# Three low bits of each 64-bit weight: from a VectorE instruction to a second GpSimd instruction

## The chip, the core and the metric

The kernel runs on one core of one Trainium2 chip. The metric is the device time of one execution in microseconds. Engines are named as the profile names them: PE is TensorE's matmul and PEld its weight load, DVE is VectorE, ACT is ScalarE, POOL is GpSimd, SP is SyncE, whose queue issues most loads.

## What is computed

Attention with a learned position bias, and behind it a feed-forward layer of two matrix products. The 2304 tokens are 4 batches of 576; there are 8 heads of 64.

```python
scores = scale * np.matmul(q, k.transpose(0, 1, 3, 2))
x = (psi_rel / psi_i)[..., None]            # from the positions alone
bias = np.maximum(x @ w1 + b1, 0.0) @ w2    # 576 x 576 for each head
scores = scores + bias.transpose(2, 0, 1)[None]
...
attn = attn / (np.sum(attn, axis=-1, keepdims=True) + 1e-09)
attn_out = np.matmul(attn, v)
...
h = x @ w_in                                # 512 -> 2048
g = h * np.clip(h + 3.0, 0.0, 6.0) / 6.0
out = g @ w_out                             # 2048 -> 512
```

The weights `w_in` and `w_out` arrive as 64-bit floats. The chip reads them as pairs of 32-bit words and builds 32-bit floats from them.

## The kernel before

**The 64-bit weights.** `w_in` is worked through in 8 chunks of 128 x 1024 numbers (`w_in_prep`), `w_out` in 8 more (`w_out_prep`). A chunk is 1 MB, and lies in SBUF as 1024 pairs (low word, high word) in each partition. One chunk takes these steps: a load on SP's queue (L242); on ACT the absolute value of the high word, scaled so that the exponent of a 64-bit float becomes that of a 32-bit one (L252, into the staging tile `u`); on POOL the high word times 0, which leaves only its sign, +0 or -0, in place (L253); and then on DVE `f64_pack`, three instructions: L260 clamps `u` and takes its maximum, L263 shifts `u` left by three bits and ORs the sign into it, L266 shifts the low word right by 29 bits and ORs its three top bits in. Then the chunk is scaled by a power of two and split into two f16 parts: the high part on ACT (L123) and the low part on DVE (L140). For the first two chunks of `w_out` POOL does two of these steps (L128, L133).

For `w_in` the chunks land in two buffers named `w` by turns, and the staging tile is the space of `wo`. For `w_out` they land by turns in two parts of `wo` and in `z_e`, and `u` is `cu`.

**What surrounds it.** The program has three stretches. First the position bias is made in 36 groups of 16 rows: z on DVE (L846) and ACT (L850), a matmul (L863), the evacuation on ACT (L879, `bo`), and a store to DRAM from ACT's queue (L885). Eight groups make the first bias table of 128 rows, which is loaded back (`bt<-bias`, L488) before the first softmax. Alongside run the eight chunks of `w_in` and the first attention tiles: the scores plus bias and the row minimum of the negative on DVE (L559), exp on ACT (L570), a transpose on PE (L618) evacuated by ACT (L621). When the last chunk of `w_in` is done, DVE computes the ratios of its rows (L216, `r_w1c`) and the first feed-forward block begins: h on PE (L781), relu on ACT (L771), the product on DVE (L764), the f16 split on ACT (L758) and POOL (L760). The eight chunks of `w_out` are made in this second stretch. Its end is the ratios of `w_out` (L216 again, `r_w2c`), with which the stored g of the first block are scaled (L121, L123); then the second product of the block begins (L804, `o_ps`). From there on, the third stretch, attention and feed-forward blocks alternate on PE to the end.

**What sets the order.** Every engine runs its instructions in the order of the program, and that order is made by a scheduler at build time from the priorities of the code and its own idea of how long things take. So a change of one instruction also moves others.

## Time and profile before

| | before |
|---|---|
| device time, median of 3 runs | 695.44 us (695.28 to 698.04) |
| span of the profiled execution, first to last instruction | 690.7 us |
| PE busy in it | 640.2 us (93%) |
| DVE busy | 486.6 us (70%) |
| ACT busy | 487.5 us (71%) |
| POOL busy | 261.1 us (38%) |

The profile is of one execution. It lists its span but no time of its own; by the median, 4.7 us lie around the span. A busy engine is one that has an instruction running; matmuls are pipelined, so a busy PE is not one at its peak. A line such as L266 is a line of the kernel before.

### The profile page before, as it was taken

The numbers are of one execution on the slowest core, as the hardware profiler recorded it, in microseconds if no ns is written. First come the engines' busy times: TensorE is split into PE (matmuls) and PEld (weight loads), VectorE is DVE, ScalarE is ACT, GpSimd is POOL, SyncE is SP. The second block draws the span as 40 slices with busy tenths as digits, with TensorE's granted clock in tenths as the row PEclk, the third lists the DMA queues.
The fourth block names the chain that finished last, engine by engine and source line by source line (L and its number), as shares of the span: only waits on it lengthen the run. The fifth ranks groups of instructions, "written<-read, shape, count | busy, mean of one in ns | idle before, by whom it ended". The sixth has DMA issues, their size and how long they took to land. (4 is left out here: it accounts for less than half of the span.)

```text
span 690.7 us, 15099 instructions
## 1 busy us (share of the span) xinstructions
PE 640.2 (93%) x5552; PEld 453.1 (66%) x5552; DVE 486.6 (70%) x1150; ACT 487.5 (71%) x970; POOL 261.1 (38%) x322
## 2 busy tenths in 40 slices
PE   7688899787899999899989999999999999999998
PEld 2234456564587667578878877777767777777775
DVE  7889977999737977577778777876688668731310
ACT  7986768987739977697568857886688657832620
POOL 1111125756114532255335634653265425420420
PEclk9998999998999999999999999999999999999999
DMA  8899769651856798979999989787968795730000
GB/s 295 297 329 345 263 246 366 234 194 32 259 162 147 188 251 178 256 180 196 237 266 232 232 186 206 149 184 154 242 123 184 159 198 120 114 66 25 1 10 28
DMA packets 175737, 130.13 MB, mean 188 GB/s; under 512 B 137520, under 2 KB 144944, under 8 KB 174640
## 3 DMA queue, kind: packets, MB, share of 16 engines
q1 hardware_dynamic: 165872, 113.84, 66.0%
q10 hardware_dynamic: 9792, 15.34, 7.4%
q8 instruction: 43, 0.70, 0.4%
q14 instruction: 30, 0.25, 0.1%
HBM read 77.24 MB, written 15.34 MB: 134 GB/s over the span
## 5 line engine op out<-in xcount | busy, mean ns | idle before, releaser
L781 PE MATMUL h_ps<-x,wi 128*128 128x256 f16 (+1 forms) x1536 | 200.9, 288 | 8.7 <-DVE t L764 6.0
L804 PE MATMUL o_ps<-g,wo 128*128 128x256 f16 (+1 forms) x1536 | 195.5, 286 | 2.0 <-ACT g L123 1.3
L781 PEld LDWEIGHTS <-wi 128*128 128x128 f16 x1536 | 147.4, 98 | 60.9 <-issue 20.1
L804 PEld LDWEIGHTS <-wo 128*128 128x128 f16 x1536 | 147.3, 98 | 47.4 <-issue 10.5
L760 POOL TENSOR_TENSOR g<-t,g 128x256 f16<-128x256 f32 (+1 forms) x128 | 105.6, 834 | 154.9 <-ACT g L758 153.4
L570 ACT ACTIVATE bt<-bt,sm 128x576 f32<-128x576 f32 x144 | 110.6, 768 | 57.0 <-DVE sm L559 53.7
L140 DVE SCALAR_TENSOR_TENSOR hl<-bt,sm,hl 128x576 f16<-128x576 f32 x112 | 99.2, 900 | 30.1 <-ACT hl L123 14.7
L764 DVE SCALAR_TENSOR_TENSOR t<-t,t,h_ps 128x320 f32<-128x320 f32 (+1 forms) x112 | 56.0, 515 | 40.3 <-ACT t L771 39.2
L117 POOL TENSOR_SCALAR hl<-bt,sm 128x576 f16<-128x576 f32 x56 | 47.4, 847 | 94.9 <-DVE sm L582 30.1
L758 ACT ACTIVATE g<-t 128x256 f16<-128x256 f32 (+1 forms) x128 | 55.4, 438 | 31.8 <-DVE t L764 30.9
L559 DVE CUSTOM_DVE_ANT_0 bt<-s_ps,bt 128x576 f32<-128x576 f32 x88 | 64.5, 751 | 10.8 <-PE s_ps L527 5.4
L771 ACT ACTIVATE t<-h_ps,t,hr 128x320 f32<-128x320 f32 (+1 forms) x112 | 64.1, 586 | 6.1 <-PE h_ps L781 4.2
L413 POOL TENSOR_TENSOR qkl<-st,qkh 128x576 fp32r<-128x576 f32 (+2 forms) x48 | 57.9, 1229 | 24.3 <-ACT qkh L406 18.6
L863 PE MATMUL b_ps<-z_e,w_sb 128*32 128x288 f32 x448 | 45.1, 430 | 12.3 <-ACT bo L879 5.1
L814 ACT ACTIVATE ot<-o_ps,os 128x256 f32<-128x256 f32 (+1 forms) x32 | 15.9, 496 | 56.6 <-PE o_ps L804 51.4
L123 ACT ACTIVATE hl<-bt,sm 128x576 f16<-128x576 f32 x56 | 43.0, 770 | 7.2 <-DVE sm L582 4.2
L578 DVE TENSOR_SCALAR sm<-sm 128x1 f32<-128x1 f32 x112 | 16.7, 150 | 44.4 <-ACT bt L570 44.0
L846 DVE TENSOR_SCALAR z_e<-T,nbp 128x576 f32<-128x576 f32 x69 | 39.6, 622 | 11.6 <-PE b_ps L863 11.5
L879 ACT ACTIVATE bo<-b_ps,cv_sb,isc 128x288 f32<-128x288 f32 (+1 forms) x54 | 35.7, 663 | 2.9 <-DMA bias<-bo 2.0
L863 PEld LDWEIGHTS b_ps<-z_e,w_sb 128*32 128x32 f32 x448 | 14.8, 111 | 32.3 <-ACT z_e L850 6.6
L253 POOL TENSOR_SCALAR w<-w 128x1024 f32<-128x1024 f32 x8 | 10.8, 1348 | 65.3 <-ACT wo L252 52.9
L850 ACT ACTIVATE z_e<-T,bp 128x576 f32<-128x576 f32 x43 | 32.4, 771 | 3.9 <-DVE bp L1037 2.9
(125 smaller groups left out, 902.1 us busy)
## 6 DMA issues: line engine op xcount, KB each, us to landing
bt<-bias SPq DMA_DIRECT2D x36, 576.0 KB, 5.3
bias<-bo ACTq DMA_DIRECT2D x36, 288.0 KB, 5.6
w<-in_w_in_dram SPq DMA_DIRECT2D x8, 1024.0 KB, 7.2
vs<-in_vp_dram SPq DMA_DIRECT2D x24, 320.0 KB, 5.0
st<-in_qk_dram SPq DMA_DIRECT2D x16, 448.0 KB, 4.5
wo<-in_w_out_dram SPq DMA_DIRECT2D x5, 1024.0 KB, 5.1
bt<-bias SPq DMA_DIRECT2D x16, 288.0 KB, 3.6
qk<-in_qkd_dram SPq DMA_DIRECT2D x8, 544.0 KB, 8.9
```

The source lines that it names most:

```text
L117: nc.gpsimd.tensor_scalar(out=out, in0=full, scalar1=scale, scalar2=1.0, op0=ALU.mult, op1=ALU.mult)
L140: nc.vector.scalar_tensor_tensor(out=out, in0=full, scalar=scale, in1=high, op0=ALU.mult, op1=ALU.subtract)
L413: nc.gpsimd.tensor_sub(out=lo[:, c:c + w], in0=t[:, c:c + w], in1=hi[:, c:c + w].bitcast(F32))
L559: nc.vector.tensor_tensor_reduce(out=halves(bt), in0=ps, in1=halves(src), op0=ALU.add, op1=ALU.min, scale=-0.125, scalar=3.0e38, accum_out ...
L570: nc.scalar.activation(out=bt, in_=bt, func=AF.Exp, scale=-1.0, bias=sm[:, 0:1], accum_out=total)
L758: nc.scalar.activation(out=g[:, 0], in_=uu, func=AF.Copy)
L760: e.tensor_sub(out=g[:, 1], in0=uu, in1=g[:, 0])
L764: nc.vector.scalar_tensor_tensor(out=t_t[f], in0=t_t[f], scalar=cols(f)[2], in1=h_t.pop(f)[:, 0:n], op0=ALU.min, op1=ALU.mult,)
L771: nc.scalar.activation(out=t_t[f], in_=h_t[f][:, 0:n], func=AF.Relu, scale=cols(f)[0], bias=cols(f)[1],)
L781: nc.tensor.matmul(out=h_t[f][:, 0:n], lhsT=wi[:, a, c, f * 128:(f + 1) * 128], rhs=x[:, e, c], start=(k == 0), stop=(k == 3 * KC - 1),)
L804: nc.tensor.matmul(out=ops[:, 0:n], lhsT=wo[:, a, f, e * 128:(e + 1) * 128], rhs=g_t[f][:, r], start=(f == 0 and a == 0 and r == 0), stop= ...
L863: nc.tensor.matmul(out=pss[a][32 * k:32 * k + 32, 0:HALF], lhsT=w2_sb, rhs=z[:, a * HALF:(a + 1) * HALF],)
```

## The change

The instruction L266 on DVE is taken out. In its place POOL gets a second instruction behind the one that makes the sign. It reads the chunk as 16-bit numbers: the upper half of the low word (`lo`, every fourth 16-bit number), multiplies it by 7.499/65535, and writes the rounded result, a number from 0 to 7, as a 16-bit number into the lower half of the high word (`low`), beside the sign. The OR of L263 then puts sign and three low bits in at once.

```diff
+LOW3 = 7.499 / 65535
...
     def f64_abs(t, u):
         if len(t.shape) == 3:
             tv, u = t.rearrange("p a (c w) -> p a c w", w=2), u.rearrange("p (a c) -> p a c", a=2)
-            lo, hi = tv[:, :, :, 0], tv[:, :, :, 1].bitcast(F32)
+            t16 = t.bitcast(U16).rearrange("p a (c w) -> p a c w", w=4)
+            lo, low, hi = t16[:, :, :, 1], t16[:, :, :, 2], tv[:, :, :, 1].bitcast(F32)
...
         nc.scalar.activation(out=u, in_=hi, func=AF.Abs, scale=F64_BIAS)
         nc.gpsimd.tensor_scalar(
             out=hi, in0=hi, scalar1=0.0, scalar2=1.0, op0=ALU.mult, op1=ALU.mult
         )
-        return lo, hi.bitcast(U32), u
-
-    def f64_pack(lo, sign, u, top):
+        nc.gpsimd.tensor_scalar(
+            out=low, in0=lo, scalar1=LOW3, scalar2=1.0, op0=ALU.mult, op1=ALU.mult
+        )
+        return hi.bitcast(U32), u
+
+    def f64_pack(rest, u, top):
         ub = u.bitcast(U32)
         nc.vector.tensor_scalar(
             out=u, in0=u, scalar1=F64_MAX, scalar2=0.0, op0=ALU.min, op1=ALU.max, accum_out=top,
         )
         nc.vector.scalar_tensor_tensor(
-            out=ub, in0=ub, scalar=3, in1=sign, op0=ALU.logical_shift_left, op1=ALU.bitwise_or
-        )
-        nc.vector.scalar_tensor_tensor(
-            out=ub, in0=lo, scalar=29, in1=ub, op0=ALU.logical_shift_right, op1=ALU.bitwise_or
+            out=ub, in0=ub, scalar=3, in1=rest, op0=ALU.logical_shift_left, op1=ALU.bitwise_or
         )
```

In the changed kernel the lines have other numbers: L256 is the absolute value on ACT, L257 the sign on POOL, L260 the new instruction on POOL, L267 the clamp on DVE, L270 the OR on DVE; most later lines stand four higher (L883 is the evacuation of a bias group, L889 its store, L854 and L850 are z on ACT and DVE, L125 and L142 the two parts of the f16 split, L563 the first step of the softmax).

**ACT, around the evacuation of the eighth bias group.** Before, from the evacuation of the sixth group to that of the ninth; `bias_97` is the first table, and its eighth store is the last row.

```order
L879 ACTIVATE bo<-b_ps,cv_sb,isc 128x576
L850 ACTIVATE z_e<-T,bp 128x576
L885 DMA bias_97<-bo 16x8x576
L879 ACTIVATE bo<-b_ps,cv_sb,isc 128x576
L850 ACTIVATE z_e<-T,bp 128x576
L850 ACTIVATE z_a<-T,bp 128x576
L885 DMA bias_97<-bo 16x8x576
L879 ACTIVATE bo<-b_ps,cv_sb,isc 128x576
L850 ACTIVATE z_a<-T,bp 128x576
L885 DMA bias_97<-bo 16x8x576
L252 ACTIVATE wo<-w_262 128x1024
L123 ACTIVATE wi<-wo,w1s 128x1024 x2
```

Now, from the same evacuation:

```order
L883 ACTIVATE bo<-b_ps,cv_sb,isc 128x576
L125 ACTIVATE wi<-wo,w1s 128x1024
L854 ACTIVATE z_e<-T,bp 128x576
L889 DMA bias_97<-bo 16x8x576
L883 ACTIVATE bo<-b_ps,cv_sb,isc 128x576
L854 ACTIVATE z_e<-T,bp 128x576
L125 ACTIVATE wi<-wo,w1s 128x1024
L854 ACTIVATE z_a<-T,bp 128x576
L889 DMA bias_97<-bo 16x8x576
L883 ACTIVATE bo<-b_ps,cv_sb,isc 128x576
L854 ACTIVATE z_a<-T,bp 128x576
L256 ACTIVATE wo<-w_263 128x1024
```

The two high parts of the first chunks' split (`wi<-wo,w1s`), which stood behind the eighth evacuation (the third `bo` of the rows), now stand ahead of it, one of them directly behind the sixth.

**DVE, one chunk of `w_out` in the second stretch.** Before, from the clamp of the sixth chunk to its L266:

```order
L260 TENSOR_SCALAR cu,w2top<-cu 128x1024
L764 SCALAR_TENSOR_TENSOR t<-t,c_120,h_ps 128x256
L578 TENSOR_SCALAR sm<-sm 128x1
L263 SCALAR_TENSOR_TENSOR cu<-cu,z_e 128x1024
L204 TENSOR_SCALAR w2p<-w2top 128x1
L578 TENSOR_SCALAR sm<-sm 128x1
L582 RECIPROCAL sm<-sm 128x1
L764 SCALAR_TENSOR_TENSOR t<-t,c_120,h_ps 128x256
L140 SCALAR_TENSOR_TENSOR wo<-cu,w2s,wo 128x1024
L266 SCALAR_TENSOR_TENSOR cu<-z_e,cu 128x1024
```

Now, from the clamp of the same chunk:

```order
L267 TENSOR_SCALAR cu,w2top<-cu 128x1024
L189 TENSOR_SCALAR hs_3373<-p_v_1203,p_w_836 128x1
L563 ISA bt,sm<-s_ps,bt 128x576
L563 ISA sm 128x1
L671 TENSOR_SCALAR r_sb<-r_sb 128x4
L563 ISA bt,sm<-s_ps,bt 128x576
L563 ISA sm 128x1
L768 SCALAR_TENSOR_TENSOR t<-t,c_120,h_ps 128x256
L206 TENSOR_SCALAR w2p<-w2top 128x1
L672 RECIPROCAL r_sb<-r_sb 128x4
L768 SCALAR_TENSOR_TENSOR t<-t,c_120,h_ps 128x256
L161 TENSOR_SCALAR w2p<-w2p 128x1
```

The OR of the chunk (L270) follows two rows further on. Between clamp and OR there are now two softmax steps, and the OR is the last instruction of the pack.

**POOL, the same chunks.** Before, from the sign of the fifth chunk to that of the sixth (`qkl` is the low part of q and k of a later tile):

```order
L253 TENSOR_SCALAR wo<-wo 128x2x512
L760 TENSOR_TENSOR g<-t,g 128x256 x2
L413 TENSOR_TENSOR qkl<-st,qkh 128x576
L413 TENSOR_TENSOR qkl<-st,qkh 128x256
L760 TENSOR_TENSOR g<-t,g 128x256
L253 TENSOR_SCALAR z_e<-z_e 128x2x512
```

Now, from the sign of the fifth chunk to the new instruction of the sixth:

```order
L257 TENSOR_SCALAR wo<-wo 128x2x512
L260 TENSOR_SCALAR wo<-wo 128x2x512
L698 TENSOR_TENSOR x<-xr,x 128x256
L764 TENSOR_TENSOR g<-t,g 128x256
L417 TENSOR_TENSOR qkl<-st,qkh 128x576
L417 TENSOR_TENSOR qkl<-st,qkh 128x256
L257 TENSOR_SCALAR z_e<-z_e 128x2x512
L260 TENSOR_SCALAR z_e<-z_e 128x2x512
```

The new instruction stands directly behind the sign of its chunk here; one x (L698) has moved from ahead of the fifth sign to behind it, and two of the three g (L764) of these rows now stand elsewhere.

## Rows read from the trace of the kernel before

**Rows 1.** The page: engines' busy time, and DVE and PE in 40 equal slices.

```profile
span 690.7 us, 15099 instructions
PE 640.2 (93%) x5552; PEld 453.1 (66%) x5552; DVE 486.6 (70%) x1150; ACT 487.5 (71%) x970; POOL 261.1 (38%) x322
...
PE   7688899787899999899989999999999999999998
...
DVE  7889977999737977577778777876688668731310
```

**Rows 2.** Busy time by stretch: busy us (instructions) of each engine, then granted clock, DMA.

```profile
core 0: us, PE busy (x) PEld busy (x) DVE busy (x) ACT busy (x) POOL busy (x), PEclk, DMA share, GB/s
0.00:38.50 38.50, 27.14 (x220) 9.50 (x220) 29.70 (x63) 33.28 (x44) 6.06 (x10) 0.96 0.86 292
38.50:91.00 52.50, 43.94 (x283) 22.95 (x283) 50.76 (x116) 40.92 (x71) 6.89 (x6) 0.93 0.86 321
...
95.00:120.00 25.00, 23.10 (x175) 14.31 (x174) 20.81 (x49) 21.48 (x43) 12.49 (x11) 1.00 0.77 279
120.00:177.00 57.00, 44.39 (x346) 30.11 (x344) 55.62 (x126) 45.90 (x84) 35.99 (x31) 0.94 0.52 164
177.00:205.00 28.00, 26.76 (x248) 21.46 (x247) 12.53 (x32) 13.41 (x25) 5.17 (x7) 1.00 0.75 218
205.00:690.70 485.70, 470.88 (x4262) 352.61 (x4258) 316.32 (x763) 330.73 (x702) 194.41 (x258) 0.99 0.74 161
```

**Rows 3.** DVE's timeline: start, us, instruction, idle before it and releaser.

```profile
38.52 0.76 DVE L559 CUSTOM_DVE_ANT_0 bt<-s_ps,bt 128x576 f32<-128x576 f32 x1 [3.24 <-DMA bt<-bias]
...
88.24 0.23 DVE L216 TENSOR_SCALAR r_w1c<-w1p,rm_w 128x4 f32<-128x4 f32 x1
...
176.31 0.22 DVE L216 TENSOR_SCALAR r_w2c<-w2p,rm_w 128x8 f32<-128x8 f32 x1
```

**Rows 4.** L266, all its instructions: durations in ns (min/median/max), first and last start.

```profile
L266 DVE SCALAR_TENSOR_TENSOR wo<-w,wo x8: 1195/1222/1300, 16.0 to 79.6; 128x1024 uint32<-128x1024 uint32 x8
L266 DVE SCALAR_TENSOR_TENSOR cu<-wo,cu x5: 1211/1219/1477, 100.1 to 158.0; 128x1024 uint32<-128x1024 uint32 x5
L266 DVE SCALAR_TENSOR_TENSOR cu<-z_e,cu x3: 1211/1215/1696, 118.1 to 165.4; 128x1024 uint32<-128x1024 uint32 x3
```

**Rows 5.** L253, the sign on POOL, the same view.

```profile
L253 POOL TENSOR_SCALAR w<-w x8: 1132/1188/1959, 11.3 to 76.2; 128x1024 f32<-128x1024 f32 x8
L253 POOL TENSOR_SCALAR wo<-wo x5: 1142/1161/2042, 94.9 to 149.4; 128x1024 f32<-128x1024 f32 x5
L253 POOL TENSOR_SCALAR z_e<-z_e x3: 1122/1184/1257, 110.0 to 157.3; 128x1024 f32<-128x1024 f32 x3
```

**Rows 6.** Groups of POOL from 95 to 177 us: busy us, mean ns, idle before.

```profile
L133 POOL TENSOR_TENSOR wo<-cu,wo 128x1024 f16<-128x1024 f32 x2 | 5.3, 2656 | 2.5 <-DMA wo<-in_w_out_dram 2.5
```

**Rows 7.** The timeline of ACT and of SP's queue, 21 to 34 us.

```profile
21.69 0.85 ACT L879 ACTIVATE bo<-b_ps,cv_sb,isc 128x576 f32<-128x576 f32 x1
...
25.31 0.83 ACT L879 ACTIVATE bo<-b_ps,cv_sb,isc 128x576 f32<-128x576 f32 x1
...
27.40 0.53 ACTq L885 DMA_DIRECT2D bias<-bo  x1
27.76 2.19 ACT L123 ACTIVATE wi<-wo,w1s 128x1024 f16<-128x1024 f32 x2
...
33.22 0.39 SPq L488 DMA_DIRECT2D bt<-bias  x1
```

**Rows 8.** DVE's timeline, 22 us: the maximum over the first V tile.

```profile
22.09 0.82 DVE L175 TENSOR_REDUCE vparts<-vf 128x1 f32<-128x640 f32 x1 [1.66 <-DMA vf<-in_vp_dram]
```

**Rows 9.** DVE and POOL side by side, at three places.

```profile
10.94 1.84 DVE L846 TENSOR_SCALAR z_e<-T,nbp 128x576 f32<-128x576 f32 x2
...
11.30 1.18 POOL L253 TENSOR_SCALAR w<-w 128x1024 f32<-128x1024 f32 x1 [10.01 <-ACT wo L252]
...
53.49 1.27 DVE L140 SCALAR_TENSOR_TENSOR wi<-wo,w1s,wi 128x1024 f16<-128x1024 f32 x1
...
54.68 1.22 DVE L266 SCALAR_TENSOR_TENSOR wo<-w,wo 128x1024 uint32<-128x1024 uint32 x1
...
54.92 1.96 POOL L253 TENSOR_SCALAR w<-w 128x1024 f32<-128x1024 f32 x1 [4.90 <-ACT wo L252]
...
55.81 2.12 DVE L140 SCALAR_TENSOR_TENSOR wi<-wo,w1s,wi 128x1024 f16<-128x1024 f32 x1
...
157.31 1.12 POOL L253 TENSOR_SCALAR z_e<-z_e 128x1024 f32<-128x1024 f32 x1
...
158.03 1.48 DVE L266 SCALAR_TENSOR_TENSOR cu<-wo,cu 128x1024 uint32<-128x1024 uint32 x1
```

**Rows 10.** PE's timeline where the second product of the first block runs.

```profile
188.25 15.88 PE L804 MATMUL o_ps<-g,wo 128*128 128x256 f16 x144 [0.70 <-DVE xr L691]
```

More of the change, by code (lines that the diff above doesn't have):

```diff
@@ L14 @@
 U32 = mybir.dt.uint32
+U16 = mybir.dt.uint16
 AF = mybir.ActivationFunctionType
@@ L247, in f64_abs @@
             tv, u = t.rearrange("p a (c w) -> p a c w", w=2), u.rearrange("p (a c) -> p a c", a=2)
-            lo, hi = tv[:, :, :, 0], tv[:, :, :, 1].bitcast(F32)
+            t16 = t.bitcast(U16).rearrange("p a (c w) -> p a c w", w=4)
+            lo, low, hi = t16[:, :, :, 1], t16[:, :, :, 2], tv[:, :, :, 1].bitcast(F32)
         else:
             tv = t.rearrange("p (c w) -> p c w", w=2)
-            lo, hi = tv[:, :, 0], tv[:, :, 1].bitcast(F32)
+            t16 = t.bitcast(U16).rearrange("p (c w) -> p c w", w=4)
+            lo, low, hi = t16[:, :, 1], t16[:, :, 2], tv[:, :, 1].bitcast(F32)
         nc.scalar.activation(out=u, in_=hi, func=AF.Abs, scale=F64_BIAS)
@@ L352, in pack @@
         def pack(k, tu):
-            f64_pack(*tu[:3], col(top, k))
+            f64_pack(*tu[:2], col(top, k))
             row_scale(col(top, k), col(pw, k), col(sw, k))
@@ L360, in pack @@
                     next(ratio[0])
-            return tu[3].rearrange("p (k e) -> p k e", k=2)
+            return tu[2].rearrange("p (k e) -> p k e", k=2)
         def split(k, u):
```

## The prediction

> **What bounds the kernel now.** I read the page first, then the busy time by stretch, then the timelines of DVE, ACT and POOL at the stretches' edges. The page shows PE busy 640.2 of 690.7 us and DVE only 486.6; taken alone that says a DVE instruction is worth nothing [rows 1]. The slices contradict the average: in the first quarter PE has sevens and DVE nines, later it is the other way round. The busy time by stretch makes that exact [rows 2]. From 38.5 to 91 us DVE is busy 50.8 of 52.5, PE 43.9, ACT 40.9. From 120 to 177 us DVE is busy 55.6 of 57, ACT 45.9, PE 44.4. In these two stretches DVE sets the pace. From 95 to 120 us it doesn't: PE has 23.1 of 25, ACT 21.5, DVE 20.8. Up to 38.5 us ACT leads with 33.3, and DVE ends the stretch waiting 3.2 us for the first bias table to come back from DRAM [rows 3]. From 188 us PE works without a gap for 15.9 us [rows 10], and from 205 to the end it is busy 470.9 of 485.7. So what happens before 177 us is a run-up, at whose end DVE delivers the ratios of w_out (176.3 us) [rows 3], and what is saved in it moves everything behind it forward, since behind it PE is full. What the change can win is PE's idle time in the run-up: 11.4, 8.6, 1.9 and 12.6 us in the four stretches named, from PE's busy times in [rows 2].
>
> **What is removed.** L266 runs 16 times, with medians of 1.215 to 1.222 us [rows 4]: 19.5 us of DVE. Successive DVE instructions overlap a little in the record (in [rows 9] L266 starts at 54.68 and the next at 55.81), so one L266 takes 1.13 us of DVE's order. Counted on DVE's timeline, three of the 16 lie before 38.5 us, five between 38.5 and 91, three between 95 and 120, five between 120 and 177. Two of the last five are stretched by what runs beside them (the maxima are 1.477 and 1.696 us); from start to next start these five take 6.4 us.
>
> **What is added.** POOL gets 16 instructions. The trace has no 16-bit integer one. The nearest row is L253: the same engine, the same two multiplications, the same 1024 numbers in steps of 8 bytes, with medians of 1.161 to 1.188 us [rows 5]. The lower bound is its shortest, 1.122 us; nothing in the rows shows POOL faster per number, so I allow nothing below. The upper bound is POOL's slowest kind on as many numbers, the two-input L133 at 2.656 us [rows 6]. I take 1.18 us, because only the type of the number differs from L253. In 120 to 177 us POOL is busy 36.0 of 57 [rows 2]; with five more instructions 41.9, which still fits into 51. The OR on DVE now waits for both POOL instructions, 2.4 us behind the ACT step. On DVE the clamp (another 1.1 us) and one to several further steps lie between in the new order, two softmax steps in the chunk shown, so I put this wait at nothing; if the cover were gone at every chunk it would cost up to 1.2 us sixteen times over. What would be queued behind a waiting OR is the softmax step that PE's transposes need.
>
> **What the new instruction disturbs.** [rows 9] show POOL and DVE in each other's way. In their middle, L253 starts at 54.92 while L266, with two inputs from SBUF, is running, and takes 1.96 instead of 1.18 us; the L140 behind it, also with two, takes 2.12 instead of 1.27 us and ends 1.05 us after POOL does. Going through all 16 L253 on the timelines, DVE is lengthened beside three of them only, by 0.9, 0.85 and 0.3 us: these are the three places of [rows 9] (1.84 us for two z that take 0.95 elsewhere, 2.12 and 1.48). The others lie beside the clamp or softmax steps, whose durations don't change. That is 2.0 us over 16, or 0.13 each. The new instructions run one step later, less often beside the clamp, so I double it to 0.26 us each: 1.3 us on the five in the last stretch.
>
> The Trainium skill has a rule on this that speaks against the change (SBUF — State Buffer, section "Who interferes with whom"): VectorE and GpSimd share one port pair, and a VectorE instruction with two SBUF inputs or in a two-port mode and a GpSimd instruction that reads SBUF shut each other out entirely. [rows 9] agree with it: the pair runs one after the other. By that rule in its worst case, every new instruction holds DVE up for its whole length; the price is worked out below, as a rival.
>
> **What is moved.** Two places matter. On ACT the two high parts of the first chunks' split now stand ahead of the evacuation of the eighth bias group. The first of them needs `w1s`, which in DVE's new order comes behind the maximum over the V tile, and that waits for its load until 22.09 us in any case [rows 8]. So ACT, which finishes the sixth evacuation at 22.5 (21.69 + 0.85), waits until about 23.1. It then has two splits of 1.1 us (2.19 for two), two z, an evacuation and another z ahead of the eighth evacuation, which I put at 28.1 to 28.9 by ACT's durations, where it now runs from 25.31 to 26.14. Its store goes out at 27.40, the load back at 33.22 [rows 7], and the first softmax step at 38.52 [rows 3]. With the evacuation done at 28.9 the store goes out at about 29.2, so the first softmax step comes at about 40.3 us: 1.8 us later. DVE has by then done the clamp of the fourth chunk (before, behind that step), but one more z is left over.
>
> **The sum.** From the first softmax step to `r_w1c` DVE saves five L266 (5.7 us), the moved clamp (1.1) less the left-over z (0.4): 6.4 us. Less the 1.8 us of the later start, `r_w1c` comes at best 4.6 us earlier. PE is busy 43.9 and ACT 40.9 of the 52.5 us there, and each waits for steps of the other, so not all of it can be had; I take the middle between nothing and 4.6, that is 2.3 us. From 95 to 120 us, where PE and ACT lead, I take nothing (bound: three L266, 3.4 us). From 120 to 177 us I take the 6.4 us less the 1.3 us of disturbance: 5.1, since DVE's 55.6 falls to about 50.5 and still stands above ACT's 45.9. Together 7.4 us, carried to the end by PE's full stretch. The profiled span of 690.7 becomes 683.3; with the 4.7 us that lie around it by the median, **688.0 us**. That is the median of the runs, 695.4, less 7.4.
>
> **The rivals.** Differences under 0.5% (3.5 us) can't be told from no change here.
> - *DVE's relief comes through whole.* Then 4.6 + 3.4 + 6.4 = 14.4 us are won: 681.0 us. For it: DVE has hardly a gap in its two stretches. Against: PE would have to close nearly half of its 34.5 us of idle time.
> - *ACT and PE take over as bounds, and the relief turns into waits on DVE.* Then 0 to 3.5 us are left: about 693.7 us. For it: ACT is at 80% in the last stretch and its steps and DVE's alternate. Against: the lead of DVE there, 9.7 us, is larger than what is taken from it.
> - *The shared port gives it back.* Sixteen new instructions of 1.18 us, each shutting DVE out for its length, are 18.9 us against the 18.1 that sixteen L266 take of its order; with the 1.8 us of the later first softmax step the time is about 698, still no difference by the bound. Against: only three of 16 L253 lengthened DVE at all.
> - *POOL becomes the bound: slower.* At 2.66 us each, eight new instructions put 21.3 us onto POOL's 48.5 in 95 to 177 us (12.5 + 36.0 in [rows 2]): 69.8. If half of its 33.5 us of waiting stays, the stretch takes 86.6 instead of 82 us; with the 1.8 us that is 6.4 more, 701.8 us. It is slower by over 0.5% from 2.3 us per instruction on (65.3 + 8 x 2.3 + 1.8 is 82 + 3.5). For it: an integer type needs converting on both sides, and no row shows that. Against: operations, count and step are those of L253, which never took over 2.05 us, the times behind DVE included.
>
> **How the numbers follow.** The forecast of 3.5 to 9.5 us won: 0.48. Whole relief: 0.12. ACT and PE take over: 0.18. The port: 0.10. POOL as the bound, or a new order that is worse in some such way: 0.12. So faster 0.60, the same 0.28, slower 0.12. The range leaves out the slower end and the edge of the whole relief: 682 to 697 us.
>
> **What would show it.** In the new profile: 16 POOL instructions of about 1.18 us; DVE's busy time lower by 17 to 20 us; the first softmax step at about 40.3 us; `r_w1c` at about 86 and `r_w2c` at about 169 us; POOL's busy share in the last stretch near 80%; PE's idle time behind `r_w2c` as before. The prediction is wrong if the new instruction takes more than 2 us, if DVE's two-input steps grow by more than 3 us in all, if the first softmax step comes much later than 40.3, or if `r_w2c` moves forward and PE then waits as much longer.

## The result, and the profile after

The changed kernel takes 701.7 us (median of 4 runs) against 695.4 for the kernel before in the same series: a ratio of 1.0118, with a 95% interval of 1.0085 to 1.0151. It is slower by about 8 us by the ratio, and by 6.3 between the medians, where 7.4 us of gain were forecast.

The page of the changed kernel, its busy times [rows 1]:

```profile
span 700.9 us, 15092 instructions
...
PE 647.5 (92%) x5552; PEld 458.5 (65%) x5552; DVE 484.2 (69%) x1134; ACT 488.5 (70%) x970; POOL 303.8 (43%) x338
```

DVE has 16 instructions fewer, and yet its busy time fell by 2.4 us only, not by the 17 to 20 of the forecast. POOL's rose by 42.7 us, where 16 instructions of 1.18 us would make 18.9. The groups of POOL say why (busy us, mean ns of one, idle before):

```profile
L260 POOL TENSOR_SCALAR w<-w 128x1024 uint16<-128x1024 uint16 x8 | 22.1, 2757 | 0.7
...
L260 POOL TENSOR_SCALAR wo<-wo 128x1024 uint16<-128x1024 uint16 x5 | 13.6, 2715 | 0.4
...
L257 POOL TENSOR_SCALAR w<-w 128x1024 f32<-128x1024 f32 x8 | 9.9, 1238 | 50.1 <-ACT wo L256 43.6 <-DVE r_sb L672 6.1 <-DVE z_a L850 0.3
...
L260 POOL TENSOR_SCALAR z_e<-z_e 128x1024 uint16<-128x1024 uint16 x3 | 7.5, 2486 | 0.2
```

L260 is the new instruction, L257 the sign (L253 before). The new one costs 2.5 to 2.8 us, more than twice the sign's price. DVE's timeline and PE's at the points of [rows 3] and [rows 10]:

```profile
41.06 0.76 DVE L563 CUSTOM_DVE_ANT_0 bt<-s_ps,bt 128x576 f32<-128x576 f32 x1 [3.80 <-DMA bt<-bias]
...
97.51 0.22 DVE L218 TENSOR_SCALAR r_w1c<-w1p,rm_w 128x4 f32<-128x4 f32 x1
...
188.43 0.22 DVE L218 TENSOR_SCALAR r_w2c<-w2p,rm_w 128x8 f32<-128x8 f32 x1
...
198.71 15.88 PE L808 MATMUL o_ps<-g,wo 128*128 128x256 f16 x144 [0.20 <-ACT ot L818]
```

The first softmax step is 2.5 us later than before, `r_w1c` 9.3, `r_w2c` 12.1, PE's long run 10.5, and the end of the span 10.2. Busy time by stretch, cut at the first softmax step, at `r_w1c`, at 120 us, at `r_w2c` and behind the first block's second product (PE, PEld, DVE, ACT, POOL; then granted clock, DMA). [rows 2] cut near the same events, but the second stretch at 91 us, 2.8 us behind `r_w1c`:

```profile
0.00:41.00 41.00, 27.96 (x214) 10.26 (x214) 32.62 (x61) 34.63 (x46) 17.43 (x14) 0.95 0.83 277
41.00:97.50 56.50, 45.64 (x270) 24.17 (x271) 44.50 (x101) 38.54 (x66) 16.62 (x10) 0.82 0.83 303
97.50:120.00 22.50, 20.68 (x146) 12.11 (x144) 16.59 (x48) 17.61 (x32) 16.30 (x10) 0.97 0.74 272
120.00:188.40 68.40, 55.83 (x425) 37.69 (x425) 61.93 (x130) 54.65 (x104) 53.23 (x40) 0.93 0.49 159
...
215.00:700.90 485.90, 471.54 (x4270) 353.07 (x4266) 315.73 (x763) 331.18 (x703) 194.87 (x258) 0.99 0.74 161
```

The tail is that of before (485.9 against 485.7 us), so the whole loss lies ahead of it. In the second row DVE, which had 1.7 us of idle time in that stretch before [rows 2], has 12; PE's granted clock there is 0.82 against 0.93.

Where DVE's relief went is seen in its groups. Three of before (up to 177 us), then the same three of after (up to 186 us):

```profile
L846 DVE TENSOR_SCALAR z_a<-T,nbp 128x576 f32<-128x576 f32 x16 | 7.6, 520 | 0.1
...
L263 DVE SCALAR_TENSOR_TENSOR cu<-cu,wo 128x1024 uint32<-128x1024 uint32 x5 | 6.8, 1361 | 0.0
...
L667 DVE TENSOR_SCALAR r_sb<-r_sb 128x4 f32<-128x4 f32 x8 | 1.8, 222 | 0.8 <-ACT bt L570 0.8
```

```profile
L850 DVE TENSOR_SCALAR z_a<-T,nbp 128x576 f32<-128x576 f32 x16 | 10.8, 718 | 0.0
...
L270 DVE SCALAR_TENSOR_TENSOR cu<-cu,wo 128x1024 uint32<-128x1024 uint32 x5 | 8.8, 1751 | 1.0 <-POOL wo L135 1.0
...
L671 DVE TENSOR_SCALAR r_sb<-r_sb 128x4 f32<-128x4 f32 x8 | 6.2, 770 | 0.4 <-ACT bt L574 0.4
```

These rows alone grew by 9.6 us. The third is four numbers per partition: it can't take 770 ns by its own work. The timeline of DVE and POOL side by side shows two of the places:

```profile
31.72 3.20 DVE L850 TENSOR_SCALAR z_a<-T,nbp 128x576 f32<-128x576 f32 x2
31.89 2.71 POOL L260 TENSOR_SCALAR w<-w 128x1024 uint16<-128x1024 uint16 x1
...
81.54 2.46 POOL L260 TENSOR_SCALAR w<-w 128x1024 uint16<-128x1024 uint16 x1
81.78 2.24 DVE L671 TENSOR_SCALAR r_sb<-r_sb 128x4 f32<-128x4 f32 x1
```

Two z steps that take 0.95 us elsewhere take 3.20, and the small step 2.24: each ends just after POOL does. The profile books such a hold as DVE's busy time, not as a wait, so the table of waits doesn't show it. By the Trainium skill (SBUF — State Buffer, section "Who interferes with whom") some DVE instructions and a POOL instruction shut each other out for their whole length; these rows agree.

The second hold can be followed on. Close behind the held step stands the softmax step for which PE waits 4.04 us, and PE then runs at a granted clock of 0.57 (84.5 to 86.3 us) and 0.73 (86.4 to 89.7): 20 matmuls of `pv_ps` take 3.39 us, and 20 more just behind them, at 1.00, take 2.53. What ACT makes of these (`xr`) is what DVE then waits for, ahead of `r_w1c`.

```profile
84.53 1.17 PE L531 MATMUL s_ps<-qk 64*128 64x288 f32 x4 [4.04 <-DVE sm L563]
...
86.36 3.39 PE L664 MATMUL pv_ps<-atf,vf 128*64 128x256 f32 x20
...
90.97 2.53 PE L664 MATMUL pv_ps<-atf,vf 128*64 128x256 f32 x20
```

```profile
91.56 0.42 DVE L695 TENSOR_TENSOR xr<-pv_ps,xr 128x256 f32<-128x256 f32 x1 [1.85 <-ACT xr L687]
94.64 0.42 DVE L695 TENSOR_TENSOR xr<-pv_ps,xr 128x256 f32<-128x256 f32 x1 [2.65 <-ACT xr L687]
```

### The profile page after: what moved, and what is told of

Read it like the earlier page. It is cut to its first block, busy times and chain, and to the rows that moved or that the text cites. A ratio compares the mean times of both kernels' runs of the same rounds, so it can differ in the third digit from the quotient of the medians.

```text
span 700.9 us, 15092 instructions
## 1 busy us (share of the span) xinstructions
PE 647.5 (92%) x5552; PEld 458.5 (65%) x5552; DVE 484.2 (69%) x1134; ACT 488.5 (70%) x970; POOL 303.8 (43%) x338
## 5 line engine op out<-in xcount | busy, mean ns | idle before, releaser
L764 POOL TENSOR_TENSOR g<-t,g 128x256 f16<-128x256 f32 (+1 forms) x128 | 107.8, 853 | 140.8 <-ACT g L762 139.0
L574 ACT ACTIVATE bt<-bt,sm 128x576 f32<-128x576 f32 x144 | 110.6, 768 | 57.2 <-DVE sm L563 53.2
L142 DVE SCALAR_TENSOR_TENSOR hl<-bt,sm,hl 128x576 f16<-128x576 f32 x112 | 99.1, 900 | 30.2 <-ACT hl L125 15.2
L563 DVE CUSTOM_DVE_ANT_0 bt<-s_ps,bt 128x576 f32<-128x576 f32 x88 | 64.6, 750 | 10.7 <-PE s_ps L531 4.4
L850 DVE TENSOR_SCALAR z_e<-T,nbp 128x576 f32<-128x576 f32 x69 | 42.0, 657 | 10.4 <-PE b_ps L867 10.3
L125 ACT ACTIVATE hl<-bt,sm 128x576 f16<-128x576 f32 x56 | 43.0, 770 | 7.1 <-DVE sm L586 4.2
L854 ACT ACTIVATE z_e<-T,bp 128x576 f32<-128x576 f32 x43 | 32.3, 769 | 7.1 <-PE b_ps L867 3.8
L883 ACT ACTIVATE bo<-b_ps,cv_sb,isc 128x288 f32<-128x288 f32 (+1 forms) x54 | 35.7, 662 | 2.1 <-PE b_ps L867 1.8
L142 DVE SCALAR_TENSOR_TENSOR x<-pv_ps,xr,x 64x320 f16<-64x320 f32 (+3 forms) x56 | 23.5, 444 | 14.9 <-ACT x L724 14.5
```

Source lines behind the costliest of these rows:

```text
L142: nc.vector.scalar_tensor_tensor(out=out, in0=full, scalar=scale, in1=high, op0=ALU.mult, op1=ALU.subtract)
L563: nc.vector.tensor_tensor_reduce(out=halves(bt), in0=ps, in1=halves(src), op0=ALU.add, op1=ALU.min, scale=-0.125, scalar=3.0e38, accum_out ...
L574: nc.scalar.activation(out=bt, in_=bt, func=AF.Exp, scale=-1.0, bias=sm[:, 0:1], accum_out=total)
L764: e.tensor_sub(out=g[:, 1], in0=uu, in1=g[:, 0])
```

## Experiments on the price of the new instruction

Theory A says that the new instruction's price and its hold on DVE cost the time; B, that the new order of instructions does, whatever it takes; C, that the relief of DVE is worth nothing, since ACT or PE take over. The times of the kernel before in these series were 692.7 to 694.4 us; every ratio is against its own series.

**A table of prices on POOL**, behind the work of the kernel before (`cut` takes 1024 numbers of a type in steps of so many of them):

```diff
+    price(cut(dst, F32, 2, 1), cut(src, F32, 2, 1))
+    price(cut(dst, U16, 4, 2), cut(src, U16, 4, 1))
+    price(cut(dst, U16, 1), cut(src, U16, 1))
+    price(cut(dst, F16, 4, 2), cut(src, F16, 4, 1))
+    price(cut(dst, F32, 2, 1), cut(src, U16, 4, 1))
+    price(cut(dst, U16, 4, 2), cut(src, F32, 2, 1))
...
```

> The kernel before with a table of GpSimd multiplications behind its work, two of each form, 128x1024 numbers each: f32 to f32 in steps of 8 bytes, 16-bit integers in steps of 8 bytes, 16-bit integers side by side, f16 in steps of 8 bytes, 16-bit integer to f32, f32 to 16-bit integer, 32-bit integers, 32-bit integer to f32. The whole is longer by the table and its own time is not read. If the integer type sets the price: f32 1.1, f16 1.1 to 1.4, all integer forms 2.3 to 2.6 us, those with one integer side between. If the place of two bytes in eight sets it: the 16-bit form side by side about 1.1 to 1.3 us, f16 in steps 2.5 us, 32-bit integers about 1.1 us.

Groups of POOL in that run; the first row from a window that holds the 16-bit pair in steps of eight bytes, the second from one that holds one instruction of the pair side by side:

```profile
L1206 POOL TENSOR_SCALAR wi<-wi 128x1024 uint16<-128x1024 uint16 x2 | 4.9, 2472 | 0.1
...
L1206 POOL TENSOR_SCALAR wi<-wi 128x1024 uint16<-128x1024 uint16 x1 | 1.0, 1043 | 0.1
...
L1206 POOL TENSOR_SCALAR wi<-wi 128x1024 f16<-128x1024 f16 x2 | 5.0, 2476 | 0.2
L1206 POOL TENSOR_SCALAR wi<-wi 128x1024 uint16<-128x1024 f32 x2 | 4.9, 2474 | 0.2
...
L1206 POOL TENSOR_SCALAR wi<-wi 128x1024 f32<-128x1024 f32 x2 | 2.3, 1152 | 0.0
...
L1206 POOL TENSOR_SCALAR wi<-wi 128x1024 uint32<-128x1024 uint32 x2 | 2.2, 1112 | 0.2
L1206 POOL TENSOR_SCALAR wi<-wi 128x1024 f32<-128x1024 uint16 x2 | 2.2, 1106 | 0.2
```

The integer type costs nothing: 16-bit numbers side by side take 1.04 us, 32-bit integers 1.11, and reading 16-bit numbers in steps of eight bytes 1.11 when the result is f32. What costs 2.47 us is a 16-bit result written in steps of eight bytes, integer or float, whatever is read. The Trainium skill (GPSIMD Engine Reference, section "Performance pitfalls for Q7 kernels") puts a limit on reads at a step of eight bytes. The reads here keep within it and indeed cost nothing. On writes that row says nothing; measured, f32 takes 1.15 us at that step and a 16-bit number more than double.

**The same instruction, written side by side:**

```diff
-            lo, low, hi = t16[:, :, 1], t16[:, :, 2], tv[:, :, 1].bitcast(F32)
+            lo, low, hi = t16[:, :, 1], t.bitcast(U16)[:, 0:t.shape[1] // 2], tv[:, :, 1].bitcast(F32)
```

> The changed kernel with its 16-bit instruction writing its 1024 numbers side by side at the start of the block instead of one in every eight bytes, so that the three bits land at wrong weights. The price table gave 1.04 us for such a write and 2.48 for that in steps of eight bytes. Theory A: 1.05 to 1.2 us per instruction in the kernel, VectorE busy 471 to 475 us, and the whole as with the f32 instruction, 688 to 695 us. If 16-bit numbers as such stretch VectorE's steps, VectorE busy is 480 us or more and the whole 697 us or more.

It took 694.5 us, ratio 1.0004 (0.9986 to 1.0023): 7 us less than the changed kernel. In the code only the place of the write moved, but the order moved with it: three steps of `w_out` stand ahead of `r_w1c` on DVE, none in the changed kernel. So these 7 us are the price and the order together. The eight instructions for `w_in` average 1.16 us, and DVE is busy 475.2 us, just past the expected 475.

**The instruction added to the kernel before**, whole and on one number in 64:

```diff
+        nc.gpsimd.tensor_scalar(
+            out=low, in0=lo16, scalar1=LOW3, scalar2=1.0, op0=ALU.mult, op1=ALU.mult
+        )
```

> The kernel before with the new GpSimd instruction added and nothing taken from VectorE (the bits are then put in twice). Theory A: the instruction takes 2.5 us, stretches VectorE's steps as in the changed kernel, and nothing pays for it: VectorE busy 500 to 510 us and the whole 705 to 714 us, more than the changed kernel. Theory B (order): 694 to 700 us, since VectorE's work is that of before. Theory C: about the changed kernel's 701 to 703 us.

> The kernel before with the new 16-bit GpSimd instruction added on one number in 64, VectorE's work kept whole: the work of before, in another order of the engines' instructions. Beside the run with the whole instruction added (717.4 us, ratio 1.033). Theory A: VectorE busy 485 to 490 us and the whole 692 to 696 us, so that the added run's 23 us are the instruction's length and its hold on VectorE. Theory B: an order that is only other already costs 5 us or more: 698 to 705 us.

Whole, 717.4 us, ratio 1.033 (1.0295 to 1.0364); tiny, 696.5 us, 1.0033 (1.0008 to 1.0058). DVE's work is the same in both, its busy time 504.2 and 486.7. So the hold costs 1.1 us of DVE for each instruction. The 21 us between the two are price and hold together with whatever the order adds, for their DVE orders part at the 32nd instruction. Theory A had the whole 3 us too low and the tiny one 0.5 us too low, and DVE's busy time right in both; theory B's ranges hold neither.

**The same on ScalarE:**

```diff
-        nc.gpsimd.tensor_scalar(
-            out=low, in0=lo, scalar1=LOW3, scalar2=1.0, op0=ALU.mult, op1=ALU.mult
-        )
+        nc.scalar.activation(out=low, in_=lo, func=AF.Copy, scale=LOW3)
```

> The changed kernel with the three low bits put beside the sign by ScalarE instead of GpSimd (nothing is left out). Theory A: VectorE keeps its relief (busy 471 to 475 us) since ScalarE holds nothing that VectorE needs; ScalarE gets 16 instructions of 1.1 to 1.3 us more, about 506 us busy; if VectorE set the pace the whole is 688 to 695 us, faster than the changed kernel. Theory C (ScalarE or the order takes over): 697 to 705 us.

716.2 us, ratio 1.0333 (1.0311 to 1.0355): no theory had it that slow. DVE keeps its relief (469.7 us), but ACT pays the same doubled price and goes from 487.5 to 520.7 us:

```profile
L260 ACT ACTIVATE w<-w 128x1024 uint16<-128x1024 uint16 x8 | 19.8, 2478 | 0.2 <-POOL w L257 0.2
```

## Experiments on the hold and on the relief

In these kernels the instruction on POOL is exchanged and DVE keeps the change. First without it; with it as a second f32 multiplication of the high word; with two of those; with the 16-bit one on one number in 64, and on every first half:

```diff
-            out=low, in0=lo, scalar1=LOW3, scalar2=1.0, op0=ALU.mult, op1=ALU.mult
+            out=hi, in0=hi, scalar1=1.0, scalar2=1.0, op0=ALU.mult, op1=ALU.mult
...
-            out=low, in0=lo, scalar1=LOW3, scalar2=1.0, op0=ALU.mult, op1=ALU.mult
+            out=low[..., :32 * low.shape[-1] // 64], in0=lo[..., :32 * low.shape[-1] // 64], scalar1=LOW3, scalar2=1.0, op0=ALU.mult, op1=ALU.mult
```

> The changed kernel without its new GpSimd instruction: the three low bits of each weight are left out, VectorE does one step per block as in the changed kernel. Theory A (price and port: the new instruction takes 2.5 us instead of the 1.18 that the forecast took, and VectorE's two-input steps stand still behind it): with both gone the relief of VectorE is kept, L671 r_sb is back near 0.22 us and L850 z_e near 0.57, r_w1c ends by 87 and the whole takes 681 to 688 us. Theory B (order: the new order of instructions on ScalarE, TensorE and the DMA queues costs the time, whatever the new instruction takes): 697 to 702 us. Theory C (the relief of VectorE is worth nothing here, ScalarE or TensorE take over): 692 to 697 us.

> The changed kernel with the new GpSimd instruction kept in place, count and size, but as a second f32 multiplication of the high word by one (what the sign instruction costs): the three low bits are left out. Theory A: the new instruction takes 1.13 to 1.2 us, GpSimd is busy about 280 us, VectorE's steps are stretched by about the 0.26 us each that the prediction charged, and the whole takes 685 to 691 us, which is the forecast with its own price. Theory B (order): 697 to 702 us. Theory C: 694 to 698 us.

> The changed kernel with two more f32 multiplications of the high word by one in place of the 16-bit instruction, so that GpSimd is held about as long (2 x 1.15 = 2.3 us against 2.5) but writes whole words: the three low bits are left out. Theory A1 (the length of the GpSimd work is what costs): like the changed kernel, 698 to 703 us. Theory A2 (the 16-bit writes of every fourth number hold what VectorE's two-input steps need): VectorE busy stays near the 473.5 us of the one-f32 run (below 477 against 484 in the changed kernel) and the whole is 690 to 696 us. Theory B (order): anything from 692 to 702 us, with VectorE busy as under A2.

> The changed kernel with its 16-bit GpSimd instruction on one number in 64 (16 of 1024): the three low bits of the other weights are left out. VectorE's relief is kept, GpSimd's new work is next to nothing, and the order of the engines' instructions is another again. Theory A (price and port alone): VectorE busy about 471 us, as without the instruction, and the whole 681 to 690 us. Theory B (the order that comes with an edit decides some 5 us either way): VectorE busy 471 us too, but the whole anywhere from 690 to 700 us, as in the run without the instruction (699).

> The changed kernel with its 16-bit instruction, in steps of eight bytes as there, on the first 512 of each 1024 numbers: the three low bits of the other half are left out. GpSimd is held about as long as by one f32 instruction (1.25 to 1.35 us). If it is the length of the GpSimd work that stretches VectorE's steps: VectorE busy 472 to 476 us as with one f32 instruction (473.5) and the whole 691 to 697 us. If it is the kind of write: VectorE busy 477 to 480 us, half way to the changed kernel's 484, at that length.

Then the change for one weight alone, with a flag `new` in `f64_abs`, and for these the instruction taken out, made f32, or written side by side as above (shown for `w_in`; for `w_out` the two flags are exchanged):

```diff
+        if not new:
+            return lo32, hi.bitcast(U32), u
...
-            return f64_abs(t, stage[:, c, fs])
+            return f64_abs(t, stage[:, c, fs], True)
...
-            return (*f64_abs(t, u), u)
+            return (*f64_abs(t, u, False), u)
```

> The change for the eight blocks of w_in alone; the eight of w_out are packed as in the kernel before. Theory A (price and port): the first stretch is lost as in the changed kernel (r_w1c near 97 us against 88) and nothing is won back behind it: 699 to 706 us. Theory B (order): 692 to 702 us with r_w1c anywhere from 89 to 97.

> The change for the eight blocks of w_out alone; w_in is packed as in the kernel before. Theory A: r_w1c near 88 us as before; the stretch from there to r_w2c, 88.1 us before and 90.9 in the changed kernel, stays within 86 to 91 us, and the whole is 692 to 698 us, since the 2.5-us instruction takes back there what VectorE is spared. Theory B (order): 692 to 702 us with r_w1c anywhere from 88 to 95.

> VectorE's third step left out for the eight blocks of w_in, with nothing on GpSimd in its place (their three low bits are left out); w_out is packed as before. If the relief of w_in is what other engines swallow: 694 to 700 us, with r_w1c at 91 us or later (88.2 before). If the order alone scatters the times: 690 to 697 us. If the relief passes through: 688 to 691 us.

> VectorE's third step left out for the eight blocks of w_out, with nothing on GpSimd in its place (their three low bits are left out); w_in is packed as before. If the relief of w_out passes through, r_w1c stays at 87 to 89 us, the long run of o_ps begins at 181 to 185 us instead of 188.3, and the whole is 685 to 690 us. If no relief passes through: 692 to 697 us, VectorE's idle time before that run 7 us or more above the 23.2 of before.

> The same for w_out, with a second f32 multiplication of the high word by one on GpSimd in the place of the new instruction (the three low bits of w_out are left out). If the relief of w_out passes through: 686 to 692 us. If not: 692 to 697 us, as with the 16-bit instruction for w_out alone (696.7).

> VectorE's third step left out for the eight blocks of w_in alone, with a second f32 multiplication of the high word by one on GpSimd in its place (the three low bits of w_in are left out); w_out as before. If other engines swallow the relief of w_in: 694 to 701 us, r_w1c at 91 us or later. If the loss of the run without an instruction (699.8) was only its order: 689 to 695 us.

> VectorE's third step left out for the eight blocks of w_out alone, with the 16-bit instruction in its place writing its numbers side by side (the three bits land at wrong weights of w_out); w_in as before. If the relief of w_out passes through at a cheap instruction: 685 to 690 us. If the 686.7 us of the f32 instruction was a lucky order: 691 to 696 us.

All of them, with busy times from the page, and `r_w1c` and the start of the last of the 192 o_ps from the timeline, each from its one profiled execution (us):

| kernel | DVE busy | POOL busy | r_w1c | last o_ps | median | ratio (95%) |
|---|---|---|---|---|---|---|
| before | 486.6 | 261.1 | 88.2 | 203.9 | - | 1 |
| changed | 484.2 | 303.8 | 97.5 | 214.3 | 701.7 | 1.0118 (1.0085-1.0151) |
| no instruction | 471.7 | 255.7 | 91.8 | 211.6 | 699.3 | 1.0066 (1.0040-1.0092) |
| 16-bit, 1 in 64 | 468.9 | 258.7 | 93.2 | 207.1 | 697.3 | 1.0066 (1.0043-1.0088) |
| one f32 | 473.5 | 274.4 | 93.3 | 204.4 | 692.9 | 0.9987 (0.9958-1.0016) |
| 16-bit side by side | 475.2 | 275.1 | 95.2 | 206.1 | 694.5 | 1.0004 (0.9986-1.0023) |
| 16-bit, first half | 470.9 | 279.7 | 98.8 | 209.9 | 698.2 | 1.0048 (1.0023-1.0073) |
| two f32 | 479.2 | 299.0 | 95.6 | 208.6 | 698.2 | 1.0083 (1.0051-1.0114) |
| w_in: 16-bit | 483.5 | 278.8 | 94.9 | 211.5 | 702.8 | 1.0112 (1.0071-1.0153) |
| w_in: no instruction | 481.1 | 255.8 | 93.3 | 209.4 | 699.8 | 1.0092 (1.0057-1.0127) |
| w_in: one f32 | 481.7 | 267.6 | 94.6 | 203.9 | 694.6 | 1.0014 (0.9989-1.0040) |
| w_out: 16-bit | 484.7 | 282.9 | 87.5 | 208.1 | 696.7 | 1.0041 (1.0025-1.0057) |
| w_out: no instruction | 480.6 | 256.1 | 88.6 | 204.7 | 693.4 | 1.0016 (0.9991-1.0042) |
| w_out: one f32 | 479.8 | 268.2 | 89.9 | 198.6 | 686.7 | 0.9903 (0.9871-0.9935) |
| w_out: side by side | 478.2 | 264.7 | 87.3 | 208.7 | 699.2 | 1.0060 (1.0015-1.0106) |

**The hold on DVE is shown; its size follows the length of the POOL instruction only roughly.** Without it, or nearly so, DVE is busy 469 to 472 us. One f32 instruction of 1.2 us adds 2 to 5 us over 16, two add 7 to 10, the 16-bit one 12 to 15, that is 0.8 to 0.95 us each. The half-length one (1.35 to 1.63 us by its groups) adds nothing that shows: less than either of its theories had, while its 698.2 us are more than the 697 that one of them gave as its most. So it isn't the kind of write: theory A2 of the two-f32 run, which wanted DVE below 477, fell too (479.2, and 698.2 us, at the edge of A1). But it isn't the length alone. With the change for one weight, eight 16-bit instructions add 2.4 us for `w_in` (483.5 against 481.1) and 4.1 for `w_out` (484.7 against 480.6), that is 0.3 and 0.5 us each, where the instruction added to the kernel before cost 1.1. A likely reason, not tested, is that the order decides which DVE steps stand beside a POOL one.

**The relief doesn't reach the end.** All kernels down to "two f32" have DVE relieved by 7 to 18 us except the changed one, and none is faster than before. The kernel without an instruction has nothing new on POOL and is still slower (ratio 1.0066): theory A had 681 to 688 us, and 699.3 lies in B's range. So does the one with 1 number in 64 (697.3 us, where A had 681 to 690), while one f32 (692.9) falls between the ranges of A and C. Busy time by stretch up to the start of the long run of o_ps (188.25 us in before), one row from each of before, the changed kernel, no instruction and one f32:

```profile
0.00:188.25 188.25, 152.58 (x1135) 86.07 (x1136) 165.06 (x374) 152.06 (x259) 63.09 (x60) 0.95 0.75 260
```

```profile
0.00:198.71 198.71, 159.72 (x1134) 91.25 (x1135) 163.55 (x363) 154.60 (x263) 107.38 (x78) 0.91 0.72 244
```

```profile
0.00:195.68 195.68, 159.54 (x1132) 91.16 (x1133) 150.49 (x364) 154.21 (x264) 58.23 (x61) 0.90 0.72 249
```

```profile
0.00:188.48 188.48, 150.76 (x1132) 86.21 (x1133) 152.68 (x364) 154.55 (x264) 77.95 (x78) 0.96 0.73 260
```

The stretch less DVE's busy time is 23.2 us of idle DVE before, 35.2 in the changed kernel, 45.2 without the instruction and 35.8 with one f32. So in the f32 kernel DVE works 12.4 us less and waits 12.6 more. In the changed kernel it works 1.5 us less and waits 12.0 more: its loss, too, is in waits. One of the f32 kernel's new waits, on ACT, eats most of what had been won by then; DVE and ACT there:

```profile
172.25 0.50 DVE L218 TENSOR_SCALAR r_w2c<-w2p,rm_w 128x8 f32<-128x8 f32 x1
```

```profile
174.93 0.83 ACT L883 ACTIVATE bo<-b_ps,cv_sb,isc 128x576 f32<-128x576 f32 x1 [2.58 <-DMA at<-hl]
175.66 0.71 ACT L125 ACTIVATE g<-g,r_w2c 128x512 f16<-128x512 f16 x1
```

`r_w2c` is there 4.1 us earlier than in [rows 3], but the scaling of `g` that needs it stands on ACT's queue behind the evacuation of a bias group, whose `bo` shares its buffers with `hl` and waits until a transpose has read one. The scaling begins 0.9 us earlier than before (176.56), and PE's long run at 188.48 instead of 188.25. A sixth buffer for `hl` would test this; SBUF has no room for it, so it wasn't tried.

**w_in and w_out differ.** `r_w1c` comes at 87.3 to 89.9 us in every kernel whose `w_in` is packed as before and has nothing new beside it, and at 91.8 to 98.8 in every one where DVE is relieved there, with or without a POOL instruction. But `r_w1c` isn't the end of the packing of `w_in`. The last low part of its split on DVE, in before (`r_w1c` follows at 88.24 us [rows 3]):

```profile
83.34 2.48 DVE L140 SCALAR_TENSOR_TENSOR wi<-wo,w1s,wi 128x1024 f16<-128x1024 f32 x2
```

The same in the kernel with `w_in` relieved and no instruction, then the first step of `w_out` on DVE, then `r_w1c`:

```profile
73.77 2.48 DVE L142 SCALAR_TENSOR_TENSOR wi<-wo,w1s,wi 128x1024 f16<-128x1024 f32 x2 [0.78 <-ACT wi L125]
...
85.06 1.22 DVE L271 TENSOR_SCALAR_CACHE_REDUCE cu<-cu 128x1024 f32<-128x1024 f32 x1 [1.62 <-ACT cu L258]
...
93.29 0.22 DVE L218 TENSOR_SCALAR r_w1c<-w1p,rm_w 128x4 f32<-128x4 f32 x1
```

In all seven kernels that relieve `w_in` and put nothing, or one instruction of at most 1.53 us in the mean, on POOL for it, the split ends 3.9 to 10.4 us earlier than before, and three or four steps of `w_out` stand ahead of `r_w1c`, where before has none. So there the relief shortens the packing, and it is the new order that puts `r_w1c` later. In the three with 16-bit or two f32 instructions for `w_in` (changed, two f32, `w_in`: 16-bit) the split ends 1.9 to 3.8 us later than before, with no such step ahead.

The run of `w_in` without an instruction came out as the theory of other engines had it (699.8 us); that with one f32, 694.6, fits both of its expectations. With the 16-bit instruction for one weight alone both totals lie where theory A had them (702.8 and 696.7 us; the second lies in B's range as well), but not all the milestones: `r_w1c` at 94.9 instead of 97, and 92.8 us from `r_w1c` to `r_w2c` instead of 86 to 91. For `w_out` the f32 kernel is the one that beats both, 686.7 us, in the range of a relief that passes through, but it leaves the three low bits of `w_out` out. It takes 10 us less than the 16-bit kernel (696.7), and that these are the price isn't shown: with the cheap side-by-side instruction the same relief gives 699.2, over both of its expectations and no faster than the 16-bit one, and without an instruction 693.4, as if no relief passed through. A version that beats both and computes every bit was not found.

**What stays open.** Kernels that differ only in a cheap POOL instruction lie 6 us apart over the whole change and 12 us apart over `w_out`, in no order of their work. Since each edit makes the scheduler set another order, the order is the likely cause: `r_w1c` stands behind 162 DVE instructions in the changed kernel and behind 175 in the one with one f32, which have the same 1134. No run holds the order to the end. Up to `r_w1c` some do: the changed kernel, the one with two f32 and the one with the 16-bit instruction for `w_in` have the same first 163 DVE instructions in the same order, and `r_w1c` at 97.5, 95.6 and 94.9 us. The first and the third have the same work there, and ACT's order in common too, and still lie 2.6 us apart; before and the four `w_out` kernels share their first 171 and lie between 87.3 and 89.9. So single executions scatter such a milestone by some 2.6 us, which hides what the slower form costs there. Nor is it shown what the granted clock adds in all. For the same matmuls up to the long run, PE is busy 152.6 us at a mean of 0.95 of the full 2.4 GHz and 159.7 at 0.91, with more of the time at 1.2 GHz.

A last table asked where the doubled price ends.

```diff
+    price_on(nc.gpsimd, cut(dst, U16, 2, 1), cut(src, U16, 4, 1))
+    price_on(nc.gpsimd, cut(dst, F32, 4, 1), cut(src, F32, 2, 1))
+    price_on(nc.vector, cut(dst, U16, 4, 2), cut(src, U16, 4, 1))
...
+    price_on(nc.scalar, cut(dst, U16, 2, 1), cut(src, U16, 4, 1))
```

> The kernel before with a second table behind its work, two of each form, 128x1024 numbers each (the whole is longer by it and its own time is not read): GpSimd writing 16-bit numbers in steps of four bytes, and f32 in steps of sixteen; VectorE writing 16-bit numbers in steps of eight and of four bytes, and f32 in steps of eight; ScalarE writing f32 in steps of eight bytes and 16-bit numbers in steps of four. If any 16-bit write that leaves part of a word pays: both steps on GpSimd and ScalarE 2.3 to 2.6 us, f32 1.1 to 1.2 us. If it is the step of eight bytes: 16-bit in steps of four 1.1 to 1.4 us. VectorE: 1.1 to 1.3 us if the price is that of the engines that paid it so far, 2.2 us or more if it is the memory's.

```profile
L1215 POOL TENSOR_SCALAR wi<-wi 128x1024 f32<-128x1024 f32 x2 | 4.1, 2054 | 0.1
...
L1215 DVE TENSOR_SCALAR wi<-wi 128x1024 uint16<-128x1024 uint16 x4 | 3.7, 1043 | 6.4 <-POOL wi L1215 6.4
...
L1215 POOL TENSOR_SCALAR wi<-wi 128x1024 uint16<-128x1024 uint16 x2 | 2.7, 1349 | 0.0
L1213 ACT ACTIVATE wi<-wi 128x1024 uint16<-128x1024 uint16 x2 | 2.7, 1348 | 0.0
L1213 ACT ACTIVATE wi<-wi 128x1024 f32<-128x1024 f32 x2 | 2.3, 1132 | 5.9 <-DVE wi L1215 5.8
```

On POOL f32 in steps of 16 bytes also costs 2.05 us, and 16-bit in steps of four bytes only 1.35, on ACT the same. Results two numbers apart are cheap, four numbers apart about double (f32 in steps of 16 bytes was not run on ACT). DVE writes 16-bit numbers at 1.04 us in the mean of both steps.

## Why the prediction was wrong

- **The step that failed first is the price of what is added**: "I take 1.18 us, because only the type of the number differs from L253." The step differed too, counted in numbers: two for L253, four here. Measured: 2.5 to 2.8 us, about the upper bound of 2.656. The prediction had named "more than 2 us" as what would make it wrong. With the write side by side (1.16 us for `w_in`), and in another order, the kernel took 7 us less.
- **What it disturbs** was put at 0.26 us each. One f32 instruction does that (0.1 to 0.3); the 2.5-us one costs 0.8 to 0.95 in the changed kernel, or 12 to 15 us instead of 4. With that, DVE's busy time hardly falls. This term was sized by L253 and fell with its price.
- **The relief passing through** failed on its own. The f32 kernel is the change at the assumed price, and it took 692.9 us, ratio 0.9987, where 688 were forecast. DVE was relieved by 13.1 us, and new waits took all of it, as the rival "ACT and PE take over" has it, given 0.18 and 693.7 us; whether those engines as bounds or the order of their queues made the waits is not shown. The argument for the gain was that DVE leads ACT by 9.7 us in the last stretch; a busy share shows a lead, but not what the next engine's order lets through. In the first stretch the middle "between nothing and 4.6" was too high: from the first softmax step to `r_w1c` (38.52 to 88.20 us before, 41.06 to 97.50 now) DVE's busy time fell from 48.2 to 44.5 us and its idle time rose from 1.5 to 11.9. Which of its waits come from the hold and which from the new order stays open: `r_w1c` came 3.6 us or more later in every kernel that relieves `w_in`, also where nothing new stood on POOL.
- **The rivals.** The time is that of "POOL becomes the bound" (701.8 us, 0.12), and its condition, 2.3 us per instruction, was met. But its mechanism wasn't seen: POOL has 15 of 68 us free from 120 to 188 us, and DVE's gaps end elsewhere: ahead of `r_w2c` its longest wait for POOL is 1.8 us in the table of waits, of 33 us that it stands idle (188.4 less 155.6). So the time is met by luck. The hold of the shared-port rival was seen, but at about a third of the instruction's length (0.8 to 0.95 of 2.5 to 2.8 us) and not the whole of it. The "new order that is worse in some such way", which the prediction put into the same 0.12, has the kernel without an instruction for it: slower than before at no price at all. How the 8 us divide among the three isn't shown.
- **Right:** the later first softmax step, 41.06 against 40.3 us, through the moved evacuation, forecast at 28.1 to 28.9 us and found at 28.01 to 28.82; the OR's wait for POOL at nothing (1.0 us in the rows of L270 above, and that for another step); POOL's share near 80% in the last stretch (53.2 of 68.4, in a longer one); and the tail, which carries any shift to the end unchanged.

## What to carry to other kernels

Price a new instruction by a row with the same step counted in numbers, and by how the result is written, not by its count and operation alone; where no row has it, two instructions behind the kernel's end cost one run. When work moves to GpSimd, part of its length can be paid on VectorE too: look for short VectorE steps that end just behind a GpSimd one, since the profile books that as busy. Before a milestone is compared between two kernels, look at what stands ahead of it in each: here `r_w1c` came later though the packing had ended earlier. And a relieved engine gains only what the next engine's order lets through: the same kernel with a neutral stand-in for the new instruction helps to tell that apart from its price, as far as the order stays the same.

## What was not expected of the hardware

- A 16-bit result in steps of eight bytes costs 2.47 us per 128x1024 on GpSimd and 2.48 on ScalarE; side by side it costs 1.04 on GpSimd, f32 in steps of eight bytes 1.15 there and 1.13 on ScalarE.
- GpSimd's f32 doubles nearly too once the step is four numbers (2.05 us at 16 bytes), while reading 16-bit numbers in steps of eight bytes costs nothing (1.11 us).
- A VectorE step of four numbers per partition (0.22 us) was held for 2.24 us beside a GpSimd instruction of 2.46.
